# Contiguous row-transform halves, re-ordered queues, first weight-gradient rows by token blocks, and weight-gradient copies on ScalarE

## The chip, the cores and the metric

The kernel runs on one core of a Trainium2 chip. Its engines work side by side, each on its own queue in order: TensorE (PE; its weight loads are listed as PEld), VectorE (DVE), ScalarE (ACT), GpSimd (POOL) and SyncE (SP). SP and POOL issue nearly all DMAs here. The metric is device time in microseconds (us), taken over several executions; the median counts. One further execution was taken with the hardware profiler, and all lines quoted below come from it.

## The reference: what is computed

The reference is a transformer-like block with its backward pass, on 2048 tokens of 1024 features, in bf16:

```python
mod = (silu(c) @ w_mod)            # six rows: sa, ca, ga, sb, cb, gb
h = layernorm(x) * (1 + ca) + sa
x = x + ga * irfft2(rfft2(h) * (w_r + 1j * w_i))
h = layernorm(x) * (1 + cb) + sb
x = x + gb * (gelu(layernorm(h) @ w1 + b1) @ w2 + b2)
out, grads = vjp(...)(grad_out)    # out and nine gradients
```

The hidden width is 3584. The gradients are those of x, w_r, w_i, w1, b1, w2, b2, c and w_mod.

## The kernel before

Both Fourier transforms are done as matmuls with cosine and sine matrices, after folds that use their symmetry (`fold_tok`, `fold_d`). Features and tokens fall into four classes CE, CO, SE, SO (even and odd frequencies of cosine and sine). `spectral_core` (L453 to L592) does one whole transform, weighting and inverse transform. It is called once forward and once backward:

- `s_fwd` (L442) transforms along the tokens, 32 matmuls for each class: tiles `pu`, result `U`.
- eight *pairs* (`pair`, L469): a pair does the row transform of 128 frequencies, in 32 matmuls of 256 columns (tiles `pcs`, L479). Two results go into one PSUM tile, to the even and to the odd columns (`po[:, st:512:2]`). Each tile is then copied (`evac_c`, L484 to L486) to `cs` in SBUF, which so holds each frequency's two parts side by side. VectorE combines `cs` to `Pt`, multiplies it with the spectral weights `ws` (L506 to L509) and adds up `R` (L512, L513). Backward, it also makes the gradient of the weights (L518 to L527). `pair_load` (L460) loads the weights of the next pair.
- `s_inv` (L531): the inverse along the tokens, with matrices `smi` that are loaded transposed from DRAM by SP, all sixteen pieces before the first pair (L551 to L556). Then the inverse along the rows: 256-column matmuls with `gm` (tiles `po`, L588), whose two halves lie side by side in PSUM. `gm` is loaded in eight transposes after the second pair (L567 to L573), and its last third is made by a negation on ScalarE (L574).
- `consume_fwd` (L679) and `consume_bwd` (L997) take each block of tokens.

The order of the stages, with their time in the profiled execution:

- 0 to 126 us: rows of `mod` (`mod_block`, L225; its operand `u_b` is made on VectorE at L210), grad_out transposed, first layernorm and folds of x (L663 to L675, with `ln_dve` for block 0), and beside it part of `ph` = w2 x grad_out (`ph_part`, L632: tiles `pp`, L638). `wt` holds two groups of w2, loaded transposed (`load_w2t`, L276).
- 126 to 370 us: the forward `spectral_core`, with more `pp` matmuls between, and the rest of `pp` behind it. The seven w1 loads of 1 MB (L707 to L709) stand behind that in the program.
- 370 to 826 us: a list written out by hand (L820 to L845) interleaves 28 `z_block`s and 8 `bo_pass`es. A z block does 32 matmuls `pz` (L748) in four tiles; ScalarE copies each with its bias (L751) and then does a Square and two Sigmoids (L752, L755, L756) for gelu and its derivative. A bo pass does hidden x w2 (`pbo`, L786), copies four tiles on ScalarE (L795), makes the output, and sums up `pa` (L804). `ordered()` holds each of these matmuls behind the one before it in program order.
- 826 to 1046 us: the gradient through w1 (`pg`, L934), the two layernorms backward, folds into `fbuf2` (L960 to L962) for the backward transform.
- 1046 to 1149 us: `fill(6)` and `fill(10)` take *pieces* (L1051), units of the weight gradients that are done whenever `fill` is called: first gw2 in 128 x 512 tiles (`gw2acc`, L1028), from hidden rows that are loaded transposed (`hh_load`, L1052; tiles `hht`, `hhsA`, `otl`) and from `gB` = grad_out x gb (L971 to L977); the tile is copied at L1033. Later gw1 (`gw1acc`, L1094, copied at L1098). There are four PSUM tiles for them. Then `s_fwd` of the backward transform, with `mid_bwd` (L1115) in its middle: it stores three rows of sums through one small row tile (`store_gmod`, L173).
- 1149 to 1495 us: backward pairs, inverse and `consume_bwd`, with pieces of gw2 between (`beside_bwd`, L1123).
- to the end: gw1, and the rows of the gradient of w_mod (`gmod_steps`, L874).

A scheduler decides the order on each engine from the program order, from priorities (`tc.high_priority()`) and from explicit orders: `tc.issue_after(x)` makes what stands under it issue after instruction x. `nc.any` lets the scheduler choose between VectorE and ScalarE. PSUM is eight tiles of 128 x 512 fp32: two each of the kinds s and d, and four of f.

Of the kernel before, what the change touches and what calls it, by code (L numbers as in the profile page):

```python
# [30 lines left out]
NB = 4  # L31
# [4 lines left out]
def kernel(  # L36
# [88 lines left out]
    def load_tok(t4, src, i, eng=None):  # L125
        s3 = tok_flat(src)
        (eng or nc.sync).dma_start(out=t4[:, 0:4:3, :],
                          in_=bass.AP(tensor=s3.tensor, offset=s3.offset + 128 * i * D, ap=[[D, P], [1024 * D, 2], [1, D]]))
        for q in range(2):
            nc.gpsimd.indirect_dma_start(out=t4[:, 1 + q, :], out_offset=None, in_=s3,  # L130
                                         in_offset=bass.IndirectOffsetOnAxis(ap=xidx[:, 2 * i + q:2 * i + q + 1], axis=0))

# [37 lines left out]
    def tt(out, a, b, op):  # L170
        nc.vector.tensor_tensor(out=out, in0=a, in1=b, op=op)  # L171
# [38 lines left out]
    nc.vector.tensor_copy(out=u_b[:], in_=bass.AP(tensor=uc.tensor, offset=uc.offset, ap=[uc.ap[0], uc.ap[1], [0, P]]))  # L210
# [27 lines left out]
    def fold_d(dst, src, tmp):  # L238
        n = src.shape[1]
        fwd = src.rearrange("p c (b w) -> p c b w", w=512)[:, :, :, 0:256]  # L240
        rev = bass.AP(tensor=src.tensor, offset=src.offset + 1023, ap=[src.ap[0], [D, n], [-512, 2], [-1, 256]])
        tv = tmp.rearrange("p c (s b w) -> p c s b w", s=2, w=256)
        tt(tv[:, :, 0], fwd, rev, ALU.add)
        tt(tv[:, :, 1], fwd, rev, ALU.subtract)
        dv = dst.rearrange("p c (a b w) -> p c a b w", b=2, w=256)
        tt(dv[:, :, :, 0, :], tv[:, :, :, 0, :], tv[:, :, :, 1, :], ALU.add)
        tt(dv[:, :, :, 1, :], tv[:, :, :, 0, :], tv[:, :, :, 1, :], ALU.subtract)
# [27 lines left out]

    def load_w2t(fg):  # L276
        nc.sync.dma_start_transpose(out=wt[:, fg % 2], in_=B_w2[fg * 256:(fg + 1) * 256, :])
# [175 lines left out]
    def spectral_core(fwd, fb, sms, em, css, pt, evac_u, evac_c, evac_v, consume, o4tag, pfs=None, fill=lambda n: None, mid=lambda: None, beside=lambda n: None):  # L453
# [4 lines left out]
        ld_in = [None]  # L458

# [9 lines left out]
        def pair(n, par, m):  # L469
            ws = ws2[:, n % 2]  # L470
            cs = css[n % 2]
            for t in range(2):
                cl = par + 2 * t
                pcs = [ps_d("pcs"), ps_d("pcs")]
                for dc in range(4):
                    po = pcs[0 if dc < 2 else 1]
                    st = dc % 2 if dc < 2 else 3 - dc
                    for h in range(2):
                        nc.tensor.matmul(po[:, st:512:2], lhsT=Us[cl][:, 2 * dc + h, m * P:(m + 1) * P],  # L479
                                         rhs=em[:, 2 * dc + h, :], start=(h == 0), stop=(h == 1))  # L480
# [32 lines left out]
            tt(R[:, rs, :, 0:DF], qa[:, 0, :, 0:DF], qa[:, 1, :, 0:DF], ALU.subtract)  # L513
# [37 lines left out]
        for par in range(2):  # L551
            smi = reg.tile([P, 2, 4, 512], BF16, name="smi", tag=("sma", "smb")[par])
            for t in range(2):
                for i in range(4):
                    nc.sync.dma_start_transpose(out=smi[:, t, :, i * P:(i + 1) * P], in_=d_SF[:, par + 2 * t, i, :])
            smis.append(smi)  # L556
        pair_load(0)
        for par in range(2):
            for m in range(4):
# [7 lines left out]
                if par == 0 and m == 1:  # L567
# [6 lines left out]
                    nc.scalar.mul(out=gm[:, 8:12, :], in_=gm[:, 4:8, :], mul=-1.0)  # L574
        s_inv(CO, smis[1])
        s_inv(SO, smis[1])
        ct = reg.tile([P, 4, 4, D], BF16, name="ct", tag=o4tag)
# [85 lines left out]
    for i in range(4):  # L663
        x4, fb = x4s[i], fbuf[:, i]
        if i == 0:
            ln_dve(x4, 0, i)
# [66 lines left out]

    def z_block(b, g0, g1):
# [3 lines left out]
        for g in range(g0, g1):  # L738
# [33 lines left out]
    def bo_pass(b, h):  # L772
# [30 lines left out]
        for i in range(4):  # L803
            nc.tensor.matmul(pa[:], lhsT=ones_bf[:], rhs=go[:, i, :], start=(i == 0), stop=(i == 3))  # L804
# [100 lines left out]

    def sums3(b, g4, p4):
# [8 lines left out]
    for b in range(NB):  # L915
# [46 lines left out]
        fold_d(fbuf2[:, b], n3u[:], ftmp)  # L962
# [17 lines left out]
    for cl in (CE, SE, CO, SO):  # L980
        nc.sync.dma_start(out=(smA2, smB2)[cl % 2][:, cl // 2], in_=d_SF[:, cl])
# [15 lines left out]
    def consume_bwd(i, o4, tmp, tmp2, n1):  # L997
# [8 lines left out]
        norm_act(n1, n1, 0, i)  # L1006
# [10 lines left out]
        fill((6, 6, 8, 8)[i])  # L1017
# [8 lines left out]

    def gw2_mm(acc, fc, h, t):
# [3 lines left out]
    def gw2_out(acc, fc, h):  # L1031
        with tc.high_priority():
            nc.any.tensor_copy(out=gwo[:, fc % 2, h * KH:(h + 1) * KH], in_=acc[:])  # L1033
# [17 lines left out]
    def pieces():  # L1051
# [35 lines left out]
        for fg in range(F // 512):  # L1087
# [3 lines left out]
            for cch in range(NDC):  # L1091
# [5 lines left out]
                with tc.high_priority():  # L1097
                    nc.any.tensor_copy(out=ob, in_=acc[:])  # L1098
# [11 lines left out]
    fill(6)  # L1110
# [78 lines left out]
```

## Time and profile before

| what | value |
|---|---|
| median of 7 executions | 1599.26 us (1590.88 to 1606.22) |
| profiled execution | 1595.78 us |
| its span, first to last instruction | 1593.7 us |
| mean granted TensorE clock | 0.967 |
| PE busy from 154 to 215 us (forward pairs) | 58.0 of 61 us |
| PE busy from 1149 to 1311 us (backward pairs) | 142.6 of 162 us |
| PE busy from 1046 to 1149 us | 90.0 of 103 us |
| HBM traffic | 170 GB/s over the span |

About 2 us of the profiled execution lie outside its span. In the lines that follow, an entry such as `L479 PE MATMUL pcs<-empf,U 128*128 128x256 bf16 x8` names the line of the code, the engine, the operation, its output and inputs by tile name (weights 128*128, moving operand 128 x 256) and how many in a row were joined to one entry; in a timeline the two numbers ahead are its start and its length in us. What stands in square brackets is the engine's idle time before it and the instruction that ended it. SPq and POOLq mark DMA issues. A line of waits reads: engine, tile and line that waited, what it waited for, then the total in us, the number of times and the longest one. Busy time and waits of an engine say nothing of their worth by themselves: a wait of an engine that has slack costs nothing.

### The profile page before, as it was taken

The numbers are of one execution on the slowest core, as the hardware profiler recorded it, in microseconds if no ns is written. First come the engines' busy times: TensorE is split into PE (matmuls) and PEld (weight loads), VectorE is DVE, ScalarE is ACT, GpSimd is POOL, SyncE is SP. The second block draws the span as 40 slices with busy tenths as digits, with TensorE's granted clock in tenths as the row PEclk, the third lists the DMA queues.
The fourth block names the chain that finished last, engine by engine and source line by source line (L and its number), as shares of the span: only waits on it lengthen the run. The fifth ranks groups of instructions, "written<-read, shape, count | busy, mean of one in ns | idle before, by whom it ended". The sixth has DMA issues, their size and how long they took to land.

```text
span 1593.7 us, 18263 instructions
## 1 busy us (share of the span) xinstructions
PE 1469.0 (92%) x6697; PEld 681.9 (43%) x6831; DVE 1076.0 (68%) x1578; ACT 718.9 (45%) x959; POOL 370.5 (23%) x427
## 2 busy tenths in 40 slices
PE   4899999979988999999899999979979979999998
PEld 2434545434433443444334444434435434444443
DVE  5982759886678778876513977877156646898833
ACT  4765456656675746666211423322512334343211
POOL 5700632111012122122111101211023321232422
PEclk8999999989999999999999999989989999999999
DMA  9952695974756676799964346496368767854995
GB/s 326 281 172 75 157 279 180 294 235 124 229 170 225 197 238 197 216 302 274 313 220 163 130 160 211 104 274 157 70 158 242 207 170 238 205 175 135 267 210 183
DMA packets 372513, 325.33 MB, mean 204 GB/s; under 512 B 224435, under 2 KB 315585, under 8 KB 372296
## 3 DMA queue, kind: packets, MB, share of 16 engines
q1 hardware_dynamic: 338680, 209.81, 50.1%
q0 software_dynamic: 33744, 114.36, 20.5%
q8 instruction: 53, 0.87, 0.2%
q14 instruction: 36, 0.29, 0.1%
HBM read 162.57 MB, written 108.05 MB: 170 GB/s over the span
## 4 chain that ended last, share of the span: by engine, by line
PE 47%; DVE 19%; issue 13%; DMA 10%; ACT 6%; SPq 3%; POOL 2%; POOLq 0%; DVEq 0%; ACTq 0%
PE gw2acc L1028 9%; PE pbo L786 8%; PE pg L934 6%; PE pz L748 4%; PE gw1acc L1094 4%; PE pp L638 4%; PE pu L447 3%; DVE ct L171 3%; PE pcs L479 3%; PE pv L540 3%; DVE got L862 2%; DMA d_gz<-gt 2%; DVE gt L171 2%; DMA out_dram<-otl 2%; DVE gn3a L867 1%
## 5 line engine op out<-in xcount | busy, mean ns | idle before, releaser
L638 PE MATMUL pp<-gBoT,wt 128*128 128x512 bf16 x876 | 204.6, 387 | 14.7 <-DMA wt<-in_B_w_dram 10.2
L934 PE MATMUL pg<-w1T,gzr 128*128 128x512 bf16 x876 | 195.2, 381 | 1.8 <-ACT gn3b L939 0.4
L1094 PE MATMUL gw1acc<-gzh,n3n 128*128 128x512 bf16 x875 | 195.5, 380 | 1.1
L638 PEld LDWEIGHTS <-wt 128*128 128x128 bf16 x896 | 89.4, 100 | 120.6 <-issue 11.9
L748 PEld LDWEIGHTS <-w 128*128 128x128 bf16 x896 | 89.1, 99 | 118.2 <-issue 16.0
L934 PEld LDWEIGHTS <-gzr 128*128 128x128 bf16 x896 | 88.0, 98 | 107.9 <-issue 3.4
L1094 PEld LDWEIGHTS <-n3n 128*128 128x128 bf16 x896 | 87.7, 98 | 103.8
L748 PE MATMUL pz<-n3Ta,w 128*128 128x512 bf16 x437 | 101.8, 389 | 8.6 <-ACT gt L751 5.4
L748 PE MATMUL pz<-n3Tb,w 128*128 128x512 bf16 x439 | 100.4, 385 | 0.4
L1028 PE MATMUL gw2acc<-gB,hhsA 128*128 128x512 bf16 x438 | 99.5, 380 | 0.5
L786 PEld LDWEIGHTS <-hhA 128*128 128x128 bf16 x608 | 60.6, 100 | 83.6 <-issue 16.1
L751 ACT ACTIVATE gt<-pz,b_col 128x512 bf16<-128x512 f32 x112 | 72.3, 685 | 29.9 <-PE pz L748 26.5
L171 DVE TENSOR_TENSOR ct<-ct 128x2048 bf16<-128x2048 bf16 x64 | 76.0, 1218 | 5.9 <-DMA d_n<-ct 4.6
L752 ACT ACTIVATE gt<-gt 128x2048 bf16<-128x2048 bf16 x28 | 53.5, 1909 | 57.3 <-DMA d_gz<-gt 57.0
L1033 ACT CAST gwo<-gw2acc 128x512 bf16<-128x512 f32 x52 | 29.6, 582 | 106.8 <-PE gw2acc L1028 91.4
L171 DVE TENSOR_TENSOR gt<-gt,gt 128x2048 bf16<-128x2048 bf16 x56 | 67.9, 1222 | 13.7 <-ACT gt L756 12.7
L1098 ACT CAST gwo<-gw1acc 128x512 bf16<-128x512 f32 x48 | 27.8, 583 | 108.4 <-PE gw1acc L1094 96.0
L755 ACT ACTIVATE gt<-gt 128x2048 bf16<-128x2048 bf16 x28 | 53.5, 1912 | 43.7 <-DVE gt L171 43.7
L1028 PE MATMUL gw2acc<-gB,hht 128*128 128x512 bf16 x251 | 58.5, 392 | 9.8 <-DVE gB L171 9.6
L1028 PEld LDWEIGHTS <-hhsA 128*128 128x128 bf16 x448 | 44.5, 99 | 51.4
L540 PE MATMUL pv<-smi,R 128*128 128x512 bf16 x249 | 56.7, 380 | 0.3
L479 PEld LDWEIGHTS <-U 128*128 128x128 bf16 x256 | 34.4, 135 | 48.8 <-issue 25.0
(306 smaller groups left out, 2584.7 us busy)
## 6 DMA issues: line engine op xcount, KB each, us to landing
d_gz<-gt POOLq DMA_DIRECT2D x28, 512.0 KB, 6.1
gzr<-d_gz SPq DMA_DIRECT2D x28, 512.0 KB, 4.6
wblk<-in_w_mod_dram SPq DMA_DIRECT2D x12, 1024.0 KB, 8.6
d_ph<-pho POOLq DMA_DIRECT2D x21, 512.0 KB, 4.3
out_dram<-otl POOLq DMA_DIRECT2D x40, 256.0 KB, 3.9
d_hh<-hhA POOLq DMA_DIRECT2D x19, 512.0 KB, 5.0
w2sD<-in_B_w_dram SPq DMA_DIRECT2D x14, 512.0 KB
w<-in_B_w_dram SPq DMA_DIRECT2D x7, 1024.0 KB, 9.5
```

Of the source, the lines that this page charges most:

```text
L171: nc.vector.tensor_tensor(out=out, in0=a, in1=b, op=op)
L479: nc.tensor.matmul(po[:, st:512:2], lhsT=Us[cl][:, 2 * dc + h, m * P:(m + 1) * P], rhs=em[:, 2 * dc + h, :], start=(h == 0), stop=(h == 1))
L540: nc.tensor.matmul(pv[:], lhsT=R[:, cl * 4 + m, :, :].rearrange("p x w -> p (x w)")[:, base:base + 255:2], rhs=smi[:, cl // 2, m, :], star ...
L638: last_pe[0] = nc.tensor.matmul(pp[:], lhsT=wt[:, fg % 2, cch, k * P:(k + 1) * P], rhs=gBoT[j][:, cch, :], start=(cch == 0), stop=(cch == ...
L748: last_pe[0] = nc.tensor.matmul(pz[:], lhsT=w1s[g][:, cch, k * P:(k + 1) * P], rhs=n3T[:, cch, :], start=(cch == 0), stop=(cch == NDC - 1))
L751: nc.scalar.activation(out=zb[:, k, :], in_=pz[:], func=ACT.Identity, bias=b1_col[:, fc:fc + 1], scale=1.0)
L752: nc.scalar.activation(out=av, in_=zb, func=ACT.Square)
L755: nc.scalar.activation(out=sg, in_=bv, func=ACT.Sigmoid, scale=2.0 * GK)
L786: last_pe[0] = nc.tensor.matmul(pbs[i][:], lhsT=hh[:, k, i * P:(i + 1) * P], rhs=wp[:, k, :], start=False, stop=(g == 6 and k == 3))
L934: nc.tensor.matmul(pgs[i][:], lhsT=gzt[g][:, k, i * P:(i + 1) * P], rhs=w1Ts[g][:, k, h * KH:(h + 1) * KH], start=(g == 0 and k == 0), sto ...
L1028: nc.tensor.matmul(acc[:], lhsT=hh_s[hh_o[fc]][:, t, :], rhs=gBs[t // 4][:, t % 4, h * KH:(h + 1) * KH], start=(t == 0), stop=(t == NT - 1))
L1094: nc.tensor.matmul(acc[:], lhsT=n3ns[t // 4][:, t % 4, cch * P:(cch + 1) * P], rhs=gz2[t // 8][:, t % 8, :], start=(t == 0), stop=(t == NT ...
```

## The change

The change does these things:

- `pcs` matmuls write contiguous halves, and the copy to `cs` interleaves them: it reads PSUM in order and writes every second bf16.
- Queues: `smi` is loaded in two sets of eight, after the loads for the pair behind the first and the second pair; `gm` is loaded after the third pair; its negation goes to VectorE after the last `R`. The w1 loads are issued after the last `w2t` load. `ln_dve` of block 0 is issued after `u_b`. The Square and the Sigmoids of a z block are issued after the last `pbo` copy. `pa` matmuls are ordered. The multiply of `gB` is issued after the fold of block 2, the first fills after the last `gB` load, the d_SF loads after the first fill. `consume_bwd` does two pieces first and its norm after the last weight-gradient copy.
- gw2's first two row blocks are done by token blocks: four tiles at once, four matmuls each for each of the four `gB` blocks, as the last two already were.
- The weight-gradient copies are on ScalarE, but for those of these first four tiles.
- `mid_bwd` copies its three rows, which lie in partitions 0, 32 and 64, with two 65-row copies, and stores them with three DMAs in a row.

In the order of issue on each engine that results, 13 `pp` matmuls move from before the forward `s_fwd` to the run behind the transform (66 to 53, and 332 to 345), and more of the `pp` copies stand on VectorE ahead of the end of the first folds (12 where 9 stood). PE's order in the z and bo stage is as before; on ScalarE, three places there have other neighbours: before it was Square 3, first Sigmoid 3, Square 4, then the `pz` copy of block 5, and now Square 3, Square 4, both Sigmoids of 3, then that copy; around the `pz` copy of block 9, and around the first `pbo` copies of the third pass, the order changes likewise by one or two operations.

```diff
@@ -478,3 +482,3 @@
                     for h in range(2):
-                        nc.tensor.matmul(po[:, st:512:2], lhsT=Us[cl][:, 2 * dc + h, m * P:(m + 1) * P],
+                        nc.tensor.matmul(po[:, st * 256:(st + 1) * 256], lhsT=Us[cl][:, 2 * dc + h, m * P:(m + 1) * P],
                                          rhs=em[:, 2 * dc + h, :], start=(h == 0), stop=(h == 1))
@@ -482,6 +486,5 @@
                 s0 = 1 + (PW if t == 0 else 0)
-                with tc.high_priority():
-                    evac_c(cs[:, t, c0:c0 + 512], pcs[0][:])
-                with tc.high_priority():
-                    evac_c(cs[:, t, s0:s0 + 512], pcs[1][:])
+                for k, o in ((0, c0), (1, s0)):
+                    with tc.high_priority():
+                        evac_c(cs[:, t, o:o + 512].rearrange("p (w s) -> p s w", s=2), pcs[k].rearrange("p (s w) -> p s w", s=2))
             Pt = Pt2[:, n % 2]
@@ -512,3 +515,3 @@
             tt(R[:, rc, :, 0:DF], qa[:, 0, :, 0:DF], qa[:, 1, :, 0:DF], ALU.add)
-            tt(R[:, rs, :, 0:DF], qa[:, 0, :, 0:DF], qa[:, 1, :, 0:DF], ALU.subtract)
+            r_in[0] = tt(R[:, rs, :, 0:DF], qa[:, 0, :, 0:DF], qa[:, 1, :, 0:DF], ALU.subtract)
             if sp_m:
@@ -550,3 +553,4 @@
         smis = []
-        for par in range(2):
+
+        def load_smi(par):
             smi = reg.tile([P, 2, 4, 512], BF16, name="smi", tag=("sma", "smb")[par])
@@ -554,4 +558,6 @@
                 for i in range(4):
-                    nc.sync.dma_start_transpose(out=smi[:, t, :, i * P:(i + 1) * P], in_=d_SF[:, par + 2 * t, i, :])
+                    with tc.issue_after(ld_in[0].ins):
+                        nc.sync.dma_start_transpose(out=smi[:, t, :, i * P:(i + 1) * P], in_=d_SF[:, par + 2 * t, i, :])
             smis.append(smi)
+
         pair_load(0)
@@ -566,3 +572,5 @@
                 beside(par * 4 + m)
-                if par == 0 and m == 1:
+                if par == 0 and m < 2:
+                    load_smi(m)
+                if par == 0 and m == 2:
                     gm = reg.tile([P, 12, 256], BF16, name="gm", tag="gm")
@@ -573,5 +581,6 @@
                                                             in_=d_E[:, 0 if fwd else 1, 2 * cl + h, :])
-                    nc.scalar.mul(out=gm[:, 8:12, :], in_=gm[:, 4:8, :], mul=-1.0)
         s_inv(CO, smis[1])
         s_inv(SO, smis[1])
+        with tc.issue_after(r_in[0].ins):
+            nc.vector.tensor_scalar(out=gm[:, 8:12, :], in0=gm[:, 4:8, :], scalar1=-1.0, scalar2=None, op0=ALU.mult)
         ct = reg.tile([P, 4, 4, D], BF16, name="ct", tag=o4tag)
@@ -665,3 +674,4 @@
         if i == 0:
-            ln_dve(x4, 0, i)
+            with tc.issue_after(u_in.ins):
+                ln_dve(x4, 0, i)
         elif i > 0:
@@ -708,3 +718,4 @@
         wtile = reg.tile([P, NDC, BW], BF16, name=f"w1_{g}", tag=W1T[g])
-        nc.sync.dma_start(out=wtile[:], in_=w1_v[:, :, g * BW:(g + 1) * BW])
+        with tc.issue_after(w2t_in[0].ins):
+            nc.sync.dma_start(out=wtile[:], in_=w1_v[:, :, g * BW:(g + 1) * BW])
         w1s.append(wtile)
@@ -733,2 +744,7 @@
 
+    last_ev = [None]
+
+    def after_ev():
+        return tc.issue_after(last_ev[0].ins) if last_ev[0] is not None else ExitStack()
+
     def z_block(b, g0, g1):
@@ -751,7 +767,10 @@
                     nc.scalar.activation(out=zb[:, k, :], in_=pz[:], func=ACT.Identity, bias=b1_col[:, fc:fc + 1], scale=1.0)
-            nc.scalar.activation(out=av, in_=zb, func=ACT.Square)
+            with after_ev():
+                nc.scalar.activation(out=av, in_=zb, func=ACT.Square)
             nc.vector.tensor_scalar(out=av, in0=av, scalar1=GC, scalar2=1.0, op0=ALU.mult, op1=ALU.add)
             tt(bv, av, zb, ALU.mult)
-            nc.scalar.activation(out=sg, in_=bv, func=ACT.Sigmoid, scale=2.0 * GK)
-            nc.scalar.activation(out=bv, in_=bv, func=ACT.Sigmoid, scale=-2.0 * GK)
+            with after_ev():
+                nc.scalar.activation(out=sg, in_=bv, func=ACT.Sigmoid, scale=2.0 * GK)
+            with after_ev():
+                nc.scalar.activation(out=bv, in_=bv, func=ACT.Sigmoid, scale=-2.0 * GK)
             nc.vector.tensor_scalar(out=av, in0=av, scalar1=6.0 * GK, scalar2=-4.0 * GK, op0=ALU.mult, op1=ALU.add)
@@ -794,3 +813,3 @@
             with tc.high_priority():
-                nc.scalar.copy(out=bo[:, i, :], in_=pbs[i][:])
+                last_ev[0] = nc.scalar.copy(out=bo[:, i, :], in_=pbs[i][:])
         tt(go, go, bo, ALU.mult)
@@ -803,3 +822,4 @@
         for i in range(4):
-            nc.tensor.matmul(pa[:], lhsT=ones_bf[:], rhs=go[:, i, :], start=(i == 0), stop=(i == 3))
+            with ordered():
+                last_pe[0] = nc.tensor.matmul(pa[:], lhsT=ones_bf[:], rhs=go[:, i, :], start=(i == 0), stop=(i == 3))
         if b == 0:
@@ -961,3 +983,3 @@
         fold_tok(n3u, ftmp)
-        fold_d(fbuf2[:, b], n3u[:], ftmp)
+        fold2_in[b] = fold_d(fbuf2[:, b], n3u[:], ftmp)
         tt(au[:], g2[:], au[:], ALU.mult)
@@ -973,5 +995,6 @@
         gb_t = reg.tile([P, 4, D], BF16, name=f"gB{b}", tag=PXT[2 + b])
-        load_tok(gb_t, grad_out, b)
+        gb_in = load_tok(gb_t, grad_out, b)
         with tc.high_priority():
-            tt(gb_t[:], gb_t[:], bcn(gb_row, 4), ALU.mult)
+            with tc.issue_after(fold2_in[2].ins):
+                tt(gb_t[:], gb_t[:], bcn(gb_row, 4), ALU.mult)
         gBs.append(gb_t)
@@ -979,4 +1002,2 @@
     smB2 = reg.tile([P, 2, 4, 512], BF16, name="smB2", tag="smb")
-    for cl in (CE, SE, CO, SO):
-        nc.sync.dma_start(out=(smA2, smB2)[cl % 2][:, cl // 2], in_=d_SF[:, cl])
     empf = reg.tile([P, 2048 + 4 * PW], BF16, name="empf", tag="wt")
@@ -1005,3 +1026,5 @@
         load_tok(n1, A_x, i)
-        norm_act(n1, n1, 0, i)
+        fill(2)
+        with tc.issue_after(gw_ev[0].ins):
+            norm_act(n1, n1, 0, i)
         tt(tmp, o4, n1, ALU.mult)
@@ -1016,3 +1039,3 @@
         store_tok(out_1, o4, i)
-        fill((6, 6, 8, 8)[i])
+        fill((4, 4, 6, 6)[i])
         for q in range(4):
@@ -1030,5 +1055,5 @@
 
-    def gw2_out(acc, fc, h):
+    def gw2_out(acc, fc, h, copy=nc.scalar.copy):
         with tc.high_priority():
-            nc.any.tensor_copy(out=gwo[:, fc % 2, h * KH:(h + 1) * KH], in_=acc[:])
+            gw_ev[0] = copy(out=gwo[:, fc % 2, h * KH:(h + 1) * KH], in_=acc[:])
         if h == 1:
@@ -1054,4 +1079,5 @@
 
-        for fc in range(2):
-            hh_load(fc)
+        hh_load(0)
+        yield
+        hh_load(1)
         for fc in range(NFC):
@@ -1059,3 +1085,14 @@
                 hh_load(fc + 2)
-            for h in range(2 if fc < NFC - 2 else 0):
+            if fc == 1:
+                first = [(f_, h, ps_f("gw2acc")) for f_ in range(2) for h in range(2)]
+                for b in range(NB):
+                    for f_, h, acc in first:
+                        for t in range(4 * b, 4 * b + 4):
+                            gw2_mm(acc, f_, h, t)
+                    if b < NB - 1:
+                        yield
+                for f_, h, acc in first:
+                    gw2_out(acc, f_, h, nc.any.tensor_copy)
+                yield
+            for h in range(2 if 1 < fc < NFC - 2 else 0):
                 acc = ps_f("gw2acc")
@@ -1097,3 +1134,3 @@
                 with tc.high_priority():
-                    nc.any.tensor_copy(out=ob, in_=acc[:])
+                    gw_ev[0] = nc.scalar.copy(out=ob, in_=acc[:])
                 nc.gpsimd.dma_start(out=out_4[cch * P:(cch + 1) * P, fg * 512:(fg + 1) * 512], in_=ob)
@@ -1109,3 +1146,7 @@
 
-    fill(6)
+    next(todo)
+    with tc.issue_after(gb_in.ins):
+        fill(6)
+    for cl in (CE, SE, CO, SO):
+        nc.sync.dma_start(out=(smA2, smB2)[cl % 2][:, cl // 2], in_=d_SF[:, cl])
     sums3(3, gn3s[1], pru)
@@ -1116,4 +1157,7 @@
         sums3_ga(3, au)
-        for k in range(3):
-            store_gmod([a[32 * k:32 * k + 1, :] for a in acc3], (3, 4, 2)[k])
+        rows = small.tile([P, D], BF16, tag="gmrow", bufs=1)
+        for h in range(2):
+            nc.vector.tensor_copy(out=rows[0:65, h * KH:(h + 1) * KH], in_=acc3[h][0:65, :])
+        for k, r in enumerate((3, 4, 2)):
+            nc.sync.dma_start(out=d_gmod[r * D:(r + 1) * D].rearrange("(o n) -> o n", o=1), in_=rows[32 * k:32 * k + 1, :])
 
```

More of the change, by code (lines that the diff above doesn't have):

```diff
@@ L126, in load_tok @@
         s3 = tok_flat(src)
-        (eng or nc.sync).dma_start(out=t4[:, 0:4:3, :],
+        ins = (eng or nc.sync).dma_start(out=t4[:, 0:4:3, :],
                           in_=bass.AP(tensor=s3.tensor, offset=s3.offset + 128 * i * D, ap=[[D, P], [1024 * D, 2], [1, D]]))
@@ L131, in load_tok @@
                                          in_offset=bass.IndirectOffsetOnAxis(ap=xidx[:, 2 * i + q:2 * i + q + 1], axis=0))
+        return ins
     def load_tok_half(t4, src, i, h):
@@ L170, in tt @@
     def tt(out, a, b, op):
-        nc.vector.tensor_tensor(out=out, in0=a, in1=b, op=op)
+        return nc.vector.tensor_tensor(out=out, in0=a, in1=b, op=op)
     def store_gmod(srcs, r):
@@ L209 @@
     uc = u_col[:]
-    nc.vector.tensor_copy(out=u_b[:], in_=bass.AP(tensor=uc.tensor, offset=uc.offset, ap=[uc.ap[0], uc.ap[1], [0, P]]))
+    u_in = nc.vector.tensor_copy(out=u_b[:], in_=bass.AP(tensor=uc.tensor, offset=uc.offset, ap=[uc.ap[0], uc.ap[1], [0, P]]))
     sb_saf = reg.tile([P, 2, D], BF16, name="sb_saf", tag="sb")
@@ L246, in fold_d @@
         tt(dv[:, :, :, 0, :], tv[:, :, :, 0, :], tv[:, :, :, 1, :], ALU.add)
-        tt(dv[:, :, :, 1, :], tv[:, :, :, 0, :], tv[:, :, :, 1, :], ALU.subtract)
+        return tt(dv[:, :, :, 1, :], tv[:, :, :, 0, :], tv[:, :, :, 1, :], ALU.subtract)
     def fold_tok(h4, tmp):
@@ L274 @@
     go_f = tok_flat(grad_out)
+    w2t_in = [None]
     def load_w2t(fg):
-        nc.sync.dma_start_transpose(out=wt[:, fg % 2], in_=B_w2[fg * 256:(fg + 1) * 256, :])
+        w2t_in[0] = nc.sync.dma_start_transpose(out=wt[:, fg % 2], in_=B_w2[fg * 256:(fg + 1) * 256, :])
     x4s = [reg.tile([P, 4, D], BF16, name=f"x4_{i}", tag=f"uv{i}") for i in range(4)]
@@ L458, in spectral_core @@
         ld_in = [None]
+        r_in = [None]
         def pair_load(n):
@@ L904 @@
     au = reg.tile([P, 4, D], BF16, name="au", tag="px1")
+    fold2_in = {}
     def sums3(b, g4, p4):
@@ L1025 @@
     gwo = reg.tile([P, 2, D], BF16, name="gwo", tag="ph")
+    gw_ev = [None]
     def gw2_mm(acc, fc, h, t):
```

## The prediction

> **What bounds the kernel now.** I read the page's first part and the chain of waits, then the list of PE's waits, then PE's busy time by stage, and last the timeline around each long wait.
>
> ```profile
> PE 1469.0 (92%) x6697; PEld 681.9 (43%) x6831; DVE 1076.0 (68%) x1578; ACT 718.9 (45%) x959; POOL 370.5 (23%) x427
> PE 47%; DVE 19%; issue 13%; DMA 10%; ACT 6%; SPq 3%; POOL 2%; POOLq 0%; DVEq 0%; ACTq 0%
> ```
>
> PE is the bound: busy for 92% of the span, and it also sets the end. So a microsecond counts if PE's matmuls get shorter, or if PE stops waiting. The list of PE's waits gives the second kind:
>
> ```profile
> PE pcs L479 <- ACT cs01b L604: 14.2, 2, 10.9
> PE pp L638 <- DMA wt<-in_B_w_dram: 10.2, 1, 10.2
> PE gw2acc L1028 <- DVE gB L171: 9.6, 3, 6.6
> PE pm L231 <- DVE u_b L210: 8.0, 1, 8.0
> ...
> PE gw2acc L1028 <- DVE gwo L1033: 4.6, 1, 4.6
> ...
> PE pcs L479 <- DVE row L176: 3.1, 1, 3.1
> ```
>
> (Columns: total us, times, longest.) A wait costs more than itself. After the 2.28 us gap at 332 us ten matmuls started 0.427 us apart where 0.216 is usual: the granted clock was halved for some 4 us. I add this loss, half of the slow stretch, to each wait below. The Trainium skill, "TensorE: Matmul & The Clock Gate", Part 1, puts the half clock behind an idle window of about 3.4 us; this trace shows it behind shorter gaps too. By the page's rule the two waits under 3.4 us that I remove would lose only themselves, and the sum below would be about 4 us smaller.
>
> The first kind is seen by comparing L479, the 256-column matmul with every second PSUM column as its output, with L588, 256 columns side by side, in two places of the timeline:
>
> ```profile
> 1150.90 1.89 PE L479 MATMUL pcs<-empf,U 128*128 128x256 bf16 x8
> 245.79 1.04 PE L588 MATMUL po<-gm,V 128*128 128x256 bf16 x8
> ```
>
> One L479 lasts 0.38 us and one L588 0.27, so the spacing is (1.89-0.38)/7 = 0.216 us against (1.04-0.27)/7 = 0.110. Both have K = 128, the same operand types and full clock; a 512-column matmul also takes 0.216-0.220. The strided output thus costs as much as 512 columns.
>
> **The change part by part** (us; + is time gained).
>
> 1. *Contiguous halves, forward.* 128 L479 matmuls x 0.106 = 13.6 of PE time. The stage (154 to 215 us) has PE busy 58.0 of 61 and DVE 44.7. With 13.6 off PE needs 44.4, so DVE's chain of tensor passes over each pair is as long. I take +10; 0 to +14. The casts to SBUF (585-590 ns on ACT) now write every second bf16. No cast here shows this. The nearest rows: weight loads that read every second bf16 (L540) take 100 ns against 98-99 for contiguous ones; casts that read PSUM backwards (L648 on ACT) take 583 against 580. On the other side stands the doubling of L479 itself, which would give 0.585 more for each of 64 casts, 37. I take 0, since the SBUF row is nearer. The Trainium skill, "SBUF — State Buffer", section "Door 1: The DMA port swizzle", also says that bf16 may be strided by up to 8 elements in SBUF for free; no run here shows it for a write by ACT.
>
> 2. *Contiguous halves, backward.* Again 13.6. From 1200 to 1260 us PE was busy 19.9 of every 20, so it is on the path. But the stage from 1149 to 1311 moves 70% DMA share; with some 35 us off it the share would be near 0.9. I keep +10; 0 to +14.
>
> 3. *gm negation and transposes.* In the timeline of the second backward pair:
>
> ```profile
> 1161.38 9.89 SPq L572 DMA_TRANSPOSE gm<-d_E  x7
> 1177.21 1.06 ACT L574 ACTIVATE gm<-gm 128x1024 bf16<-128x1024 bf16 x1 [13.61 <-DMA gm<-d_E]
> 1178.64 1.08 ACT L604 CAST cs01b<-pcs 128x512 bf16<-128x512 f32 x2
> 1179.28 3.57 PE L479 MATMUL pcs<-empf,U 128*128 128x256 bf16 x8 [10.95 <-ACT cs01b L604]
> ```
>
> ScalarE stands at L574 until eight transposes of gm have landed; the gw2 and pcs casts queue behind it, PE runs out of PSUM. The negation goes to VectorE behind the last R, where gm has long landed, at about 0.5 us (L879, as many elements: 0.49); only po waits for it. Removed: 11.2 + 3.9 of half clock = 15.1. The transposes, 16 of smi too, are spread behind pairs 0, 1 and 2 on SP; each set of 8 takes SP about 10 us, and the next pair's loads are now ahead of it, but later hht transposes are behind it. I allow 3 for that: +12; +5 to +15.
>
> 4. *Weight-gradient casts and norm_act order.* At 1301 us ACT begins four norms (4.64 us), whose input landed late, and PSUM is full: PE waits 4.6 for a cast that VectorE finishes among its tensor ops, then 3.2 for cs01b. With half clock: 4.9+3.4+2.1+1.2 = 11.6. The norm is now held behind a gw2 cast, and the cast is on ScalarE. The norm may still stand before the last pair's casts, so +8; 0 to +12. Moving 12 VectorE casts to ACT costs nothing: in those stages ACT is busy 39% or less, and the casts wait for PE.
>
> 5. *mid_bwd rows.* Six 1-row copies with a DMA between them become two 65-row copies (0.68 each) and three DMAs. The first pcs waited 3.1 for them, plus 3.0 of half clock: +5; +2 to +6.
>
> 6. *gw2's first rows by token blocks.* From 1045 to 1058 us PE lost 13.2 (waits 1.1, 6.7, 0.6, 2.5; half clock 2.3) because gB2 and gB3 were issued at 1044.13 and 1051.83, behind hht transposes that held SP for 12.9 and 5.3. Now SP has gB0, one hht, gB1, au, gB2, n3u, gB3, then the other hht. w1T's px4 and px5 come free at about 1031 and 1035 (seven groups of 3.5 us before 1045), so all gB can be issued by 1037 and, at 13 us to landing, be there at 1050. But three hht are now behind them, and fc 1 needs the second, at 1045 or later. The blocks give 3.5 us of work for each gB. I expect 6 lost: +7; 0 to +13.
>
> 7. *w1 loads behind the last w2t.* The last w2t was issued at 344.12, after a w1 load that waited for ACT until 343.65. Its buffer is free only at about 342.7, so the order itself gives 1; the load took 16 us against a median of 10.5, with PE cover of 32 matmuls (6.9). Five earlier w1 loads went at 228-233 and now come right behind it: six MB, at 300 GB/s 3.3 us each. The first z block needs w1_0 6.9 us after w2t. I expect a wait of 6 in all instead of 10.3 + 2.9: +5; -8 to +12.
>
> 8. *z and pbo order on ACT.* Square and the sigmoids (1.91 us each) are placed after the last pbo copies. In the issue order, three places change (436, 495, 608 us in the old timeline, where PE already waits): one or two more such operations stand ahead of a pz eviction. -3; -8 to +2.
>
> 9. *Start.* 13 pp matmuls (2.8) go from before s_fwd, where they filled, to the run after; two more VectorE casts (0.69 each) go before the fold's end, which s_fwd waits for: -3; -6 to 0. u_b ahead of the statistics ends an 8.0 us wait, but the next pm waits for wblk (6.1 in 4 waits) and DMA share is 0.98 in the first 40 us: 0; 0 to +1. Ordered pa and the d_SF loads behind the fill: 0, since smA/smB are used 50 us later; if late, s_fwd would wait 2-5.
>
> Sum: 10+10+12+8+5+7+5-3-3 = +51. From the profiled execution's 1595.8 (span 1593.7): **1545**. It lies 3.5 below the median of the seven runs (1599.3), which would make 1548. As the gains of 2, 3 and 4 lie in one stage with a DMA floor, I round up: **1550**.
>
> **Rivals.**
>
> - *Pair stages bound elsewhere.* DVE (forward) and DMA (backward) already fill 73% and 70%; PE's 20 us of parts 1 and 2 turn into idle PE. For: pairs are one chain of DVE passes. Against: PE 100% busy in 1200-1260. 1570.
> - *Strided casts twice as slow.* 64 x 0.585 = 37, about 30 of it where PE waits for one of two PSUM tiles: 1580. Against: the L540 row.
> - *The halves don't do what they say:* 0.216 is due to something else (the loads L479 PEld mean 135 ns against 99): parts 1 and 2 give 0: 1570. Against: L588.
> - *Slower: the z stage's ScalarE order.* If each of blocks 3 to 16 (14) had all three 1.91 us operations ahead of its pz eviction, PE, which has four banks of 1.73 us, would lose up to 5.7 per block, 80 in all: 1630. It decides against the change from 51/14 = 3.6 us per block. For: four waits of that kind stand there now. Against: the order changes in three places only, by one or two operations.
>
> **How the numbers follow.** Forecast (1532 to 1562) 0.58; pair stages bound elsewhere 0.18; strided casts 0.07; halves without effect 0.06; slower 0.06; the rest between, within 8 us of before (0.5%, what can be told from no change), 0.05. The range of 1525 to 1585 takes in the first four and the bounds of parts 6 and 7. Faster by over 0.5%: 0.89; within: 0.05; slower: 0.06.
>
> **What would show it.** L479's x8 group at about 1.04 us and PE busy down by some 27 us; casts of cs01b still at 0.585; no PE wait for cs01b at 10 us; the gB waits at under 7; the wt wait at 5, perhaps one of pz for w1. The forecast is wrong if PE busy falls but the pair stages keep their lengths of 61 and 162 us, if the strided casts show over 0.7 us, or if pz's waits for ACT (5.4) grow past 20.

## The result, and the profile after

The changed kernel takes 1585.41 us (median of 19 runs, 1576.59 to 1592.28) against 1598.85 in runs of the kernel before beside it: a ratio of 0.9916 (95% interval 0.9901 to 0.9931), some 13 us faster. The forecast was 1550, some 49 below the median of before, and 1585.41 lies just above the stated range of 1525 to 1585. The profile that came with this result fell on a disturbed execution of 1601.42 us, so all lines of the changed kernel below are from a second one (1584.29 us, span 1582.2).

From the page's first part and the list of PE's waits:

```profile
PE 1445.3 (91%) x6697; PEld 670.0 (42%) x6831; DVE 1067.8 (67%) x1565; ACT 730.0 (46%) x968; POOL 363.0 (23%) x427
```
```profile
PE pz L764 <- ACT gt L767: 26.8, 5, 8.8
PE pv L543 <- DVE R L172: 15.1, 2, 10.7
...
PE gw2acc L1053 <- DMA hht<-d_hh: 10.0, 1, 10.0
PE gw2acc L1053 <- DMA otl<-d_hh: 7.2, 1, 7.2
PE pcs L483 <- ACT cs01b L613: 6.2, 8, 2.4
```

PE is busy for 23.7 us less, close to the 27 that the halves promised. All the long waits of before are gone from the head of the list (10.9 for cs01b, 10.2 for w2t, 6.6 for gB, 4.6 for gwo). But others stand in their place: ScalarE in the z stage, R in the pairs, hidden rows (`hht`, `otl`) twice. So PE's work got shorter and PE waits longer.

The groups of the pair matmuls and of the copies (count, then busy us and mean ns, then the idle time before them). The counts give 16 matmuls for each of the eight pairs of a pass, where the description of the kernel says 32:

```profile
L483 PE MATMUL pcs<-em,U 128*128 128x256 bf16 x128 | 18.7, 279 | 2.0 <-ACT cs L610 1.3 <-DVE cs L610 0.6
L483 PE MATMUL pcs<-empf,U 128*128 128x256 bf16 x128 | 17.9, 272 | 6.2 <-ACT cs01b L613 6.2
L613 ACT CAST cs01b<-pcs 128x512 bf16<-128x512 f32 x32 | 21.5, 745 | 0.6
```

A 256-column matmul fell from 415 and 451 ns to 279 and 272, as `po` had (278). From start to start their median is 0.109 us where it was 0.216. The interleaving copy takes 745 ns on ScalarE, not 587 (the five that VectorE made 736, not 693).

Where the time went, by the first start of each stage's first tile in the two traces (us):

| stage | before | after | gained | forecast (its parts) |
|---|---|---|---|---|
| to the first forward pcs | 154.4 | 148.8 | +5.7 | -3 (9) |
| forward pairs, to po | 60.9 | 54.5 | +6.4 | +10 (1) |
| po, rest of pp, to pz | 154.5 | 144.2 | +10.3 | +5 (7) |
| z stage, to pg | 458.0 | 469.7 | -11.7 | -3 (8) |
| pg, to gw2 | 217.0 | 217.8 | -0.8 | 0 |
| gw2's first tiles, to pu | 71.5 | 71.8 | -0.3 | +7 (6) |
| backward s_fwd | 32.6 | 29.4 | +3.2 | +5 (5) |
| backward pairs, to po | 189.7 | 186.4 | +3.3 | +30 (2, 3, 4) |
| po, gw2, gw1, to the end | 255.1 | 259.6 | -4.6 | 0 |

Up to pz the change does more than was forecast, 22 us. Then it gives 12 back, and the largest item, the backward pairs, yields a tenth. The sum of the forecast exceeds what this profile gained by 39.5 us; the pairs make 26.7 of them, the z stage 8.7, gw2's first tiles 7.3.

### The profile page after: what moved, and what is told of

Same layout as the page of the kernel before. It is cut to its first block, busy times and chain, and to the rows that moved or that the text cites. A ratio compares the mean times of both kernels' runs of the same rounds, so it can differ in the third digit from the quotient of the medians.

```text
span 1599.4 us, 18272 instructions
## 1 busy us (share of the span) xinstructions
PE 1445.1 (90%) x6697; PEld 671.2 (42%) x6831; DVE 1067.3 (67%) x1565; ACT 729.2 (46%) x968; POOL 362.3 (23%) x427
## 5 line engine op out<-in xcount | busy, mean ns | idle before, releaser
L647 PE MATMUL pp<-gBoT,wt 128*128 128x512 bf16 x874 | 197.8, 379 | 3.8 <-DMA wt<-in_B_w_dram 1.7
L764 PEld LDWEIGHTS <-w 128*128 128x128 bf16 x896 | 89.5, 100 | 140.3 <-issue 39.5
L767 ACT ACTIVATE gt<-pz,b_col 128x512 bf16<-128x512 f32 x112 | 72.9, 683 | 43.1 <-PE pz L764 37.8
L543 PE MATMUL pv<-smi,R 128*128 128x512 bf16 x250 | 62.4, 403 | 27.5 <-DVE R L172 15.0
L1135 ACT CAST gwo<-gw1acc 128x512 bf16<-128x512 f32 x56 | 32.6, 583 | 119.5 <-PE gw1acc L1131 114.0
L1053 PE MATMUL gw2acc<-gB,hht 128*128 128x512 bf16 x250 | 57.7, 390 | 11.8 <-DMA hht<-d_hh 10.5
L1053 PE MATMUL gw2acc<-gB,otl 128*128 128x512 bf16 x187 | 46.5, 406 | 10.8 <-DMA otl<-d_hh 10.6
## 6 DMA issues: line engine op xcount, KB each, us to landing
wblk<-in_w_mod_dram SPq DMA_DIRECT2D x12, 1024.0 KB, 11.7
```

Source lines behind the costliest of these rows:

```text
L543: nc.tensor.matmul(pv[:], lhsT=R[:, cl * 4 + m, :, :].rearrange("p x w -> p (x w)")[:, base:base + 255:2], rhs=smi[:, cl // 2, m, :], star ...
L647: last_pe[0] = nc.tensor.matmul(pp[:], lhsT=wt[:, fg % 2, cch, k * P:(k + 1) * P], rhs=gBoT[j][:, cch, :], start=(cch == 0), stop=(cch == ...
L764: last_pe[0] = nc.tensor.matmul(pz[:], lhsT=w1s[g][:, cch, k * P:(k + 1) * P], rhs=n3T[:, cch, :], start=(cch == 0), stop=(cch == NDC - 1))
L767: nc.scalar.activation(out=zb[:, k, :], in_=pz[:], func=ACT.Identity, bias=b1_col[:, fc:fc + 1], scale=1.0)
L1053: nc.tensor.matmul(acc[:], lhsT=hh_s[hh_o[fc]][:, t, :], rhs=gBs[t // 4][:, t % 4, h * KH:(h + 1) * KH], start=(t == 0), stop=(t == NT - 1))
L1135: gw_ev[0] = nc.scalar.copy(out=ob, in_=acc[:])
```

## Experiments

The queue theory, formed on the first profile of the changed kernel: in the backward pairs PE isn't the bound, since VectorE's in-order queue holds passes of the pairs behind steps that wait for DMA. The rivals are the prediction's: PE is the bound there, or DMA share is. All runs stand beside runs of the kernel before.

**The changed kernel again** (no edit).

> The changed kernel as it is, for a second profile, since the first one was 16 us longer than the median. Queue theory: the strided PSUM write is gone in both passes (256 matmuls 0.109 us apart), the time to the first pz is about 22 us shorter than before, but the stages behind it give none of their expected gains: z stage about 5 to 12 us longer, backward pairs not shorter, although their matmuls need 13.8 us less. PE theory (the prediction's): in an undisturbed profile the backward pairs take 25 to 35 us less than before, and the long waits of the first profile are gone. Both: 0.99 of before.

1584.29 us, 0.9933 (0.9904 to 0.9962). This run left the profile of the table above: the first pz comes 22.3 us earlier, the z stage is 11.7 longer and the pairs gain 3.3, as the queue theory had it. The 25 to 35 us in the pairs didn't come.

**The halves alone**, on the kernel before: the matmul's output and `evac_c` as in the diff, nothing else.

> The kernel before with the contiguous halves alone (matmul output and copies to cs). PE theory: minus 20 to 27 us in all, half of it in the backward pairs. Queue theory: minus 8 to 14, nearly all in the forward pairs, since the backward pairs are paced by something else. If the strided copies cost more on ScalarE: cs01b copies above 0.7 us and less than 8 gained.

1593.83 us, 0.9984 (0.9959 to 1.0008). The backward pairs take 189.5 us against 189.7, with some 13 us of PE work less and nothing gained. The view of busy time by stretch (stretch, its length, PE, PEld, DVE, ACT, POOL busy with counts, granted clock, DMA share, GB/s) shows it, the kernel before and then the halves alone:

```profile
1148.95:1338.63 189.68, 169.99 (x754) 82.14 (x770) 105.79 (x151) 59.91 (x99) 57.23 (x62) 0.95 0.74 202
```
```profile
1145.92:1335.41 189.49, 157.27 (x753) 75.99 (x769) 105.52 (x151) 62.23 (x99) 56.55 (x62) 0.92 0.78 196
```

The forward pairs give 2.5, po to pz 1.8; the z stage gives 3.9 back. The prediction had parts 1 and 2 at +20. The 8 to 14 us of the queue theory didn't come either. What did come is the third case of the expectation: copies of 742 ns, and less than 8 us gained. So this run alone can't tell VectorE's queue from the longer copies; the next ones can.

**Rows 3 and 4 moved.** In the timeline of VectorE, after, near the end of the pairs, steps of the w_mod gradient stand ahead of the pair's first pass (`Pt`):

```profile
1280.65 0.49 DVE L899 TENSOR_SCALAR otl<-otl,u_rt 128x1024 bf16<-128x1024 bf16 x1 [3.84 <-DMA out_dram<-otl]
1283.83 0.49 DVE L899 TENSOR_SCALAR otl<-otl,u_rt 128x1024 bf16<-128x1024 bf16 x1 [2.69 <-DMA out_dram<-otl]
1287.00 0.49 DVE L899 TENSOR_SCALAR otl<-otl,u_rt 128x1024 bf16<-128x1024 bf16 x1 [2.69 <-DMA out_dram<-otl]
1287.40 1.29 DVE L172 TENSOR_TENSOR Pt<-cs01b 128x1028 bf16<-128x1028 bf16 x2
```

Each takes 0.49 us and waits about 3 for the store of the one before, which uses the same single buffer. This `Pt` is the seventh pair's, whose four copies to `cs01b` had ended at 1265.9, 21.5 us before. The eighth pair's copies ended at 1282.1, its `Pt` follows at 1298.3, and PE's wait of 10.7 for its R ends at 1306.2. The same steps stand there in the kernel before, six of them from 1281 to 1299 us, and PE is then busy with gw2 matmuls:

```profile
1281.00 0.49 DVE L879 TENSOR_SCALAR otl<-otl,u_rt 128x1024 bf16<-128x1024 bf16 x1 [6.11 <-DMA out_dram<-otl]
...
1299.21 0.49 DVE L879 TENSOR_SCALAR otl<-otl,u_rt 128x1024 bf16<-128x1024 bf16 x1 [2.68 <-DMA out_dram<-otl]
1299.61 1.29 DVE L171 TENSOR_TENSOR Pt<-cs01b 128x1028 bf16<-128x1028 bf16 x2
```
```profile
1283.95 13.80 PE L1028 MATMUL gw2acc<-gB,hhsA 128*128 128x512 bf16 x62
```

In the list of VectorE's waits of the changed kernel these three are for the rows in the pairs (but for 0.7 of the second):

```profile
DVE otl L901 <- DMA otl<-in_w_mod_dram: 36.5, 8, 10.2
DVE otl L899 <- DMA out_dram<-otl: 24.8, 10, 5.2
DVE otl L899 <- DMA otl<-d_gmod: 11.3, 2, 6.9
```

Three kernels take these 16 steps out of the backward pairs, the changed one, the one before, and the one before with the halves (from `beside_bwd` and from the end of the program):

```diff
-            if k < (0, 2, 2, 2, 2, 2, 3, 3)[n]:
-                with tc.issue_after(hh_in[0].ins):
-                    next(rows34[side[0] // NDC])
-                side[0] += 1
...
-    for r in (2, 1, 0):
+    for r in (4, 3, 2, 1, 0):
         gmod_row(r, w1g["ins"])
-        fill(8)
+        fill(5)
```

> The changed kernel with rows 3 and 4 of the gradient of w_mod moved out of the backward pairs, to the run of gw1 with the other rows. DVE-queue theory (each of these 16 steps waits on VectorE for the store of the one before, and the pair's passes stand behind it): the waits of PE for R and cs01b in the pairs go, the stage from first backward pcs to first po falls from 186 us by 12 to 20, and if the tail takes the rows without loss the kernel is 8 to 18 us faster than the changed one. DMA theory (the pairs are bound by DMA share): the stage falls by less than 6.

> The kernel before with the same move of rows 3 and 4 alone. DVE-queue theory: the stage of the backward pairs, 190 us, falls by only 5 to 12, since PE with its strided matmuls is the next bound. It is the base of the next kernel.

> The kernel before with the rows moved and with the contiguous halves. DVE-queue theory: the halves are now worth more in the backward pairs than the 0.2 us they were worth with the rows there: 6 to 13 us between this stage and that of the kernel with the rows moved alone. DMA theory or a wait elsewhere: under 4.

The changed kernel: 1563.31 us, 0.9784 (0.9753 to 0.9816), 21 less than unmoved. Its pairs take 163.1 us, 23.3 less, somewhat more than the 12 to 20 expected. The kernel before: 1589.80, 0.9964 (0.9939 to 0.9988), pairs 177.8. With the halves: 1581.46, 0.9896 (0.9863 to 0.9929), pairs 170.5. So the same halves, with the same longer copies, are worth 0.2 us in this stage with the rows there and 7.3 without, and the rows cost 12 before the change and 23 after it. VectorE's first wait in the changed kernel with the rows moved shows who paces now:

```profile
DVE Pt L172 <- ACT cs01b L613: 78.6, 8, 20.1
```

In all eight pairs VectorE now waits for its input, and `Pt` starts within 0.2 us of the end of the pair's copies, as it does in every kernel without these steps on VectorE. In the changed kernel it started 6.2 to 21.5 us late in six of the eight pairs, in the kernel before only in two (2.9 and 14.8).

**The rows' traffic without VectorE's part.** Moving the rows also moved 8 MB of DMA. Here the DMAs stay (loads of w_mod, stores of a row as loaded) and VectorE's two operations per step are left out, so those rows of the w_mod gradient aren't computed.

```diff
-    rows34 = [gmod_steps(r, gmy[:, 0:1], gmy[:, 1:2], sacc) for r in (3, 4)]
+    rows34 = [row_traffic(r) for r in (3, 4)]
```

> The changed kernel with the DMAs of rows 3 and 4 left in the backward pairs, as many bytes in each direction, but with VectorE's part of these 16 steps left out (the row as loaded is stored, and the sums over it stay zero). Theory that VectorE's queue paces the pairs: the stage from first backward pcs to first po is 160 to 170 us, as with the rows moved (163). Theory that the rows' DMA traffic or SP's and POOL's queues pace them: 180 to 190, as in the changed kernel.

1565.86 us, 0.9823 (0.9784 to 0.9862). The three stages, in the view of busy time by stretch; the changed kernel, then with the rows moved, then with their traffic alone:

```profile
1136.00:1322.00 186.00, 160.78 (x753) 76.25 (x767) 104.71 (x150) 57.15 (x97) 54.74 (x62) 0.94 0.79 199
```
```profile
1132.00:1295.00 163.00, 155.38 (x755) 75.25 (x768) 79.76 (x102) 58.10 (x97) 41.72 (x46) 0.99 0.75 185
```
```profile
1134.00:1303.00 169.00, 155.52 (x753) 75.15 (x766) 79.81 (x102) 57.93 (x96) 51.64 (x62) 0.97 0.91 227
```

With all the traffic in the pairs the DMA share rises to 0.91 and the stage still takes 169: about 17 of the 23 us were VectorE's part. The other 6 go with the traffic or its place in the queues of SP and POOL: PE waits 10.6 us for the hidden rows (`otl`) here and 4.7 with the rows moved. They aren't clear of the spread either, since the six variants of the changed kernel with the rows moved and gm's loads left behind the third pair take 163.1 to 167.8 us in the pairs. A DMA share of 0.79 was no bound.

**The order in the z stage undone** (`with after_ev():` taken away three times).

> The changed kernel without the order of Square and Sigmoids behind the pbo copies. Queue theory: the z stage gets 5 to 11 us shorter and the whole kernel 4 to 11 us faster than the changed one (about 1576). Rival, the z stage is longer only because its loads of w1 come later or the profile was disturbed: no difference within 3 us.

1578.54 us, 0.9904 (0.9876 to 0.9932), 6 less than the changed kernel, with intervals that overlap; z stage 465.9 against 469.7. But with the rows moved as well, the same edit gave nothing:

> The changed kernel with rows 3 and 4 moved out of the backward pairs and without the order of Square and Sigmoids. If the two effects add up (21 and 6 us): 1555 to 1560. If the z order was only worth something by chance: within 3 us of the kernel with the rows moved (1563).

1564.63, 0.9791 (0.9746 to 0.9836), where 1563.31 stood without it; z stage 469.6 and 463.8. Kernels with one and the same order here vary by nearly 7 (463.4 to 470.0 in five profiles), so a cost of this order isn't shown.

**The w1 loads back, and then all of the z stage back**, with the rows moved: `issue_after(w2t_in[0].ins)` taken away; then also `after_ev` and the ordered `pa`.

> The changed kernel with the rows moved, and the w1 loads where they were before (five early, one ahead of the last w2t load). Prediction's step 7 with what the traces showed: the last w2t is late again, pp waits about 10 us, pz starts about 10 us later than at 349. If the z stage is then also about 8 us shorter (460), the early start was given back and the kernel is within 3 us of the kernel with the rows moved; else 7 to 10 slower.

> The same, and also the order of Square and Sigmoids and of the pa matmuls as before: all that the change did to the z stage is undone. If these orders make the stage longer: 458 to 462. If it is the earlier arrival alone: 464 to 470, or by how much later pz starts shorter.

1571.37 (0.9832, 0.9796 to 0.9867) and 1565.78 (0.9818, 0.9778 to 0.9858). With the w1 loads back PE waits 6.3 for the last w2t instead of 1.7, and po to pz takes 150.2 instead of 144.4: the order is worth 5.8 there, and the whole kernel is 8 slower. pz starts at 353.4 and 356.2, the z stage takes 466.9 and 463.6. With all of the change to it undone the stage is not back at 458. Over the 17 profiles of the study it is longer the earlier it starts, from 458.0 (start at 369.9) and 461.9 (364.0) to 461.9 to 470.0 (347.5 to 349.3); a straight line gives a third of a microsecond per microsecond. PE's longest wait in it is the same in all kernels that come early. In the changed kernel, in ScalarE's and PE's timelines:

```profile
413.62 1.91 ACT L769 ACTIVATE gt<-gt 128x2048 bf16<-128x2048 bf16 x1 [11.93 <-DMA d_gz<-gt]
```
```profile
423.38 1.86 PE L764 MATMUL pz<-n3Ta,w 128*128 128x512 bf16 x4 [8.81 <-ACT gt L767]
```

A Square waits 11.93 us for the store of its tile's last use, two blocks ago, and the `pz` copies of L767 that PE needs stand behind it on ScalarE. Such waits of PE are 5.4 us before, 21 to 27 in the kernels that come 14 to 22 us earlier. That they come from the earlier arrival is argued from this relation, not shown; the kernels that start late also lack most of the change.

**The loads in front of gw2.** SP's and PE's timelines after:

```profile
1024.92 8.28 SPq L127 DMA_DIRECT2D gB<-in_grad_out_dram  x1
1033.25 16.18 SPq L1078 DMA_TRANSPOSE hht<-d_hh  x3
```
```profile
1047.00 5.30 PE L1053 MATMUL gw2acc<-gB,hht 128*128 128x512 bf16 x12 [10.03 <-DMA hht<-d_hh]
```

The last gB is issued at 1024.92 instead of 1051.83, 17 us earlier when the stage's own start (10 earlier) is taken off, as forecast; and now the second `hht` comes too late: about 13 us are lost with the half clock, as before. Two kernels ask whether it is the place of one load (asked for with the first), or the order of the matmuls (tile by tile again, on the kernel with the rows moved and the z order free):

> The changed kernel with the second load of hidden rows asked for with the first, ahead of n3u and the last gB on SP's queue. If the 10 us wait of gw2's first rows for hht is one load's place in the queue: it falls to under 5, and the kernel gains 4 to 7. If the whole of these loads is bound by DMA (about 7 MB in 25 us): the wait moves to gB and the kernel stays within 2.

> The same as the first of this set, but with the first two row blocks of gw2 tile by tile again instead of by token blocks. Prediction's step 6: the token blocks are worth 5 to 10 us, so this is slower by that. DMA theory (about 7 MB have to land before the fourth block, whatever the order of the matmuls): within 3 us, PE waits about 10 to 13 in all in either order.

1585.61 (0.9927, 0.9901 to 0.9953) and 1563.52 (0.9776, 0.9733 to 0.9820). With the earlier load the wait for `hht` falls to 6.6, and one of 1.2 for gB and one of 7.0 for a copy come up; the stage gets longer, 79.3 us for 71.8, though the median is the same. Tile by tile the wait is gB's again, 8.5 in all, and the median 1 us from that of the token blocks. So neither order gains or loses clearly. That PE waits until all of these loads have landed, whatever their order, fits the second run better than the first, whose longest wait is for a copy, and isn't shown.

**Copies on either engine** (`nc.any.tensor_copy` for `nc.scalar.copy`), on the changed kernel and on the one with rows moved and z order free.

> The changed kernel with the weight-gradient copies left to either engine again. Theory that a copy on ScalarE, waiting for the store of its gwo tile, holds the pv copies behind it: the wait of pv for ScalarE (12 us in the first profile) goes and the kernel is 5 to 12 us faster than the changed one. Prediction's step 4: 3 to 8 us slower, since a copy then stands among VectorE's passes again.

> The same as the first of this set, but with the weight-gradient copies left to either engine. With the rows gone VectorE has room, so within 3 us; if a copy among VectorE's passes still holds PE: slower by 3 to 8.

1583.63 (0.9924, 0.9897 to 0.9950): neither the gain nor the loss that was expected. In its profile a wait of 12.9 us for a gwo copy behind VectorE's row steps stands in the pairs in place of most of PE's wait for R (4.1 for 15.1). With the rows moved 1558.20 (0.9747, 0.9702 to 0.9792) against 1564.63: 6 us faster, where no gain was expected. The intervals overlap, but the place of it agrees in both: from the first po to the end it takes 255.4 and 255.5 us with free copies, 259.6 and 260.5 without.

**gm's transposes spread** over pairs 3 to 6. After, SP's and PE's timelines:

```profile
1173.34 7.08 SPq L580 DMA_TRANSPOSE gm<-d_E  x5
1180.52 2.49 SPq L1078 DMA_TRANSPOSE otl<-d_hh  x1
```
```profile
1185.08 5.10 PE L1053 MATMUL gw2acc<-gB,otl 128*128 128x512 bf16 x13 [7.17 <-DMA otl<-d_hh]
```

```diff
-                if par == 0 and m == 2:
-                    gm = reg.tile([P, 12, 256], BF16, name="gm", tag="gm")
-                    for cl in range(4):
+                if par * 4 + m in (2, 3, 4, 5):
+                    if m == 2 and par == 0:
+                        gm = reg.tile([P, 12, 256], BF16, name="gm", tag="gm")
+                    for cl in (par * 4 + m - 2,):
```

> The same with gm's eight transposes spread, two behind each of pairs 3 to 6, instead of eight behind pair 3. If these transposes on SP's queue are what makes PE wait 5 to 7 us for a load of hidden rows in the third pair: that wait falls under 2 and 4 to 8 us are gained on the kernel without the spread. If the load is late for another cause (its slot is freed late): no change within 2.

> All that looked useful together: the changed kernel with the rows moved, gm's transposes spread, copies on either engine, Square and Sigmoids free. If gm's spread takes away the wait for hidden rows in the third pair (one profile showed a stage 10 us shorter, the times 1 us): 1550 to 1555; if the wait only moves: 1558.

1563.57 (0.9779, 0.9729 to 0.9829; one of its six executions took 3872.88 us, and the other five have a median of 1562.45) and, with free copies too, 1556.91 (0.9747, 0.9712 to 0.9782). The wait for `otl` is gone in both profiles and the pairs take 156.8 us, 10.5 and 8.6 less than without the spread. The medians fell by 1 to 2 only. In both profiles some 6 us of it come back behind the pairs (from the first po to the end 266.7 for 260.5, and 261.4 for 255.5); why, and where the rest went, stays open. The last kernel, changed as it was but with rows moved, z order and copies free and gm spread, is 2.5% faster than before, 28 us faster than the changed one.

## Why the prediction was wrong

- *What failed:* parts 2, 3 and 4, "+10", "+12" and "+8" in the backward pairs, gave 3.3 in all. The step was the reading of the 1200 to 1260 us stretch: "PE was busy 19.9 of every 20, so it is on the path". It is true of that stretch, but soon after it VectorE holds a pair's passes behind six row steps, while gw2 matmuls from the same store of work keep PE busy. The prediction looked at what PE waited for, and never at VectorE's waits for `otl`, of which its own fence shows nothing. It also ended the stage at the last pcs. Up to there the stage did shrink, from 162.3 to 145.1 us; but po needs VectorE's last R too, and that starts 169.9 us after the first pcs, where it was 170.7 before (143.3 with the rows moved).
- *Its signs of being wrong:* two came true, strided casts over 0.7 us (0.745) and pz's waits for ACT past 20 (26.8). The third, pair stages that keep their lengths, looked at the last pcs and so missed what happened.
- *The rival of pair stages bound elsewhere* was nearest in kind: PE's saved work did turn into idle PE. But it named DMA at 0.7 of a share as the bound, and a stage with DMA at 0.91 took 169 us.
- *Part 3* was right in what it took away: the 10.9 wait for L574 is gone. It was replaced in part at once: the allowance of 3 for hidden rows behind gm's transposes measured 7.2, and some 2 of half clock behind it.
- *Part 1:* the matmul was sized right (0.109). The copies weren't free: 745 ns for 587, a quarter of the doubling that was the other end. With the rows moved PE's waits for cs01b come to 2.1 us in all. The Trainium skill, "SBUF — State Buffer", section "Door 1: The DMA port swizzle", lets bf16 stride for free up to 8 elements; for this write by ScalarE the runs show 27% more. Why the forward pairs gave 6.4 of the 10 with the whole change and 2.5 with the halves alone wasn't taken apart.
- *Part 6:* the gB loads came as early as forecast, but the second `hht`, which the first token block needs, came 10.0 us too late: 0 for +7. The prediction saw this load coming late and put the loss at 6 in all, where it was about 13.
- *Part 4:* copies on ScalarE cost 4 to 5 us behind the pairs, where 0 was forecast.
- *Part 8* had the place and the sign (-3 for -11.7), but by luck as far as the runs show: the order isn't shown to matter, and undoing it doesn't bring the stage back. Its cause stays open.
- *Parts 5 and 7* were right (+3.2 for +5; the loads' order measured 5.8 for 5), part 9 too gloomy: the 2.8 of pp matmuls do move, and the stages to the first pcs still took 5.7 less.

## What to carry to other kernels

Before PE time is cut in a stage, look for what the other in-order queues wait for in it: here a step of 0.5 us with a single buffer, which waits 3 us for the store of the one before, paced everything that stood behind it on its engine, and PE's filler work (the gw2 matmuls) hid much of that until PE got faster. A stage whose engine is 100% busy for a while need not be bound by that engine for all of its length; move the suspect out and see whether the cut is then worth more (here 7.3 us instead of 0.2). An earlier arrival at a stage that reuses buffers behind their stores may be given back in part; here that is argued, not shown.

## What the runs showed of the hardware

- ScalarE's copy of 128 x 512 from PSUM took 745 ns with every second bf16 as its output, 587 with contiguous ones; VectorE's 736 and 693.
- A 256-column matmul whose output is every second fp32 column of PSUM had the spacing of a 512-column one, 0.216 us; side by side 0.109.
- The granted clock in the pairs was 0.94 with the row steps, 0.97 with their traffic alone, 0.99 without them. In the changed kernel's pairs, matmuls started 0.427 us apart instead of 0.216 for a while after a wait of 2.37 us (at 1232 us), and not after one of 2.27 (at 1214 us).
